# The first forty microseconds of a fused RWKV and feed-forward kernel: a section in written order, dummy products, small loads two at a time, a new list of steps

## The chip, the cores and the metric

The kernel runs on one core of a Trainium2 chip, as one program. The metric is the device time of one execution in microseconds; the time before is the median of three runs. The engines are TensorE (PE, with its weight loads shown as PEld), VectorE (DVE), ScalarE (ACT), GpSimd (POOL) and SyncE (SP), which issues nearly all transfers. All five run their own instruction streams and wait for each other by semaphores.

## What is computed

The reference runs a linear recurrence (RWKV5) over 4 batches, 8 heads, 768 steps and a head size of 48, and feeds its output to a multiplicative feed-forward block:

```
for t in range(S):
    cur = einsum('bhd,bhe->bhde', u * k[t], v[t])
    y[t] = einsum('bhd,bhde->bhe', r[t], state + cur)
    state = w * state + einsum('bhd,bhe->bhde', k[t], v[t])
x = y.transpose(0, 2, 1, 3).reshape(3072, 384)
out = ((x @ w1) * (x @ w2) @ w3) @ w_out
```

The recurrence's inputs are float32. The four weight matrices (384 x 1024 twice, 1024 x 1024, 1024 x 384) arrive as 64-bit floating point words, and the kernel turns them into float32 by integer and shift steps on DVE and ACT.

## The kernel before

**Units.** Time is cut in 6 chunks of 128 steps; a chunk of one batch is a unit n (24 units, unit 0 to 3 are chunk 0). A unit loads k, r and v (three transfers of 192 KB in pieces of 192 bytes), scales k and r by powers of w (`scale`, letter k in the list: one DVE multiplication of 128x768), turns them (T and R: four transposes each on PE with a copy on ACT, t and r; or, for later units, DVE's block transpose x, a transfer to scratch memory y, four transfers back z and a copy l), and makes the pairwise products inside the chunk. U are the additions to the state (32 PE instructions), A the products of r and k (32), S the contribution of the carried state (24 or 48), V the contribution of the pairs (48), Y the copy of the result into `xT`. On DVE, d, e and f make the diagonal term with u, i and j update the state, m masks the products; ACT or DVE (g or h) places the diagonal, and o and p spread the state into a block form.

**Feed-forward.** For each chunk of 512 tokens and each of 8 column blocks j, a.c.j is x @ w1 and b.c.j is x @ w2 (three products of 128x512 each, or 128x256 in two parts for the first blocks), c copies a, u multiplies. w3 and w_out are first multiplied together (G, K, F, X); the last product is done with seven half-size products instead of eight (s and B for the sums, P for the products, E for gathering, D for the store).

**Weights.** W fetches one piece into one of three raw buffers (`raws`); M, N, H, L and Q convert it (ACT, DVE, DVE, ACT, DVE). Pieces 0 to 7 are strips of w1 and w2 in turn; 8 to 15 are w_out; 16 to 31 w3.

**The first section.** Before the units begin, the kernel loads w, computes powers of w up to 32 in both directions in the tile `both`, turns them on PE (`ps_p`, line 274) and copies them to `pn_in` (line 275), by which every unit is scaled. It also tests whether all of w lies in [0.6, 1.6]: a flag that each engine reads, and a branch: inside the range the program runs the list (`program(True)`), outside it another, general path. Only the list is taken here. In the kernel before, w is loaded once more as a row, and DVE takes its minimum and maximum for the flag. The order of this section is left to the scheduler of the language.

**The list.** `ORDER` is a hand-over of an order: a text of steps such as `kr.2 v.2 d.0 W.2`, letter, unit or block, part. `listed()` emits them one by one with the schedule fixed, so each engine executes its own steps in exactly this order, and a step whose input is late holds up all later steps of its engine. Loads (kr, v, W), the turn's transfers (y, z) and the stores (D) all stand in SP's queue in list order.

The buffers that set when transfers can start: three for k and r (`krin`), three for v (`vnat`), three for raw weights (`raws`), two for the scaled k and r (`krs`), two for the turned r (`tts`).

Of the kernel before, what the change touches and what calls it, by code (L numbers as in the profile page):

```python
# [8 lines left out]
F32 = mybir.dt.float32  # L9
# [7 lines left out]
PSUM = bass.MemoryType.PSUM  # L17
PE, ACT, DVE, SP = (getattr(mybir.EngineType, x) for x in ("PE", "Activation", "DVE", "SP"))
# [4 lines left out]
kr.2 v.2 d.0 W.2 N.0 e.0 f.0 M.0 k.0 g.0 H.0 U.0 kr.3 d.1 T.0 k.1 L.0 R.0 e.1 kr.4 t.0 i.0 f.1 r.0 T.1 W.3 Q.0 p.0 A.0  # L23
M.1 h.1 j.0 S.0 t.1 d.2 R.1 k.2 m.0 r.1 R.2 kr.5 e.2 U.1 N.1 r.2 f.2 A.1 M.2 H.1 T.2 i.1 L.1 m.1 V.0 d.3 p.1 W.4 Q.1
v.3 Y.0 t.2 j.1 S.1 g.2 N.2 A.2 k.3 V.1 H.2 R.3 kr.6 Y.1 U.2 m.2 M.3 v.4 T.3 N.3 L.2 a.0.0.0 k.4 r.3 W.5 i.2 a.0.1.0
H.3 p.2 c.0.0.0 e.3 L.3 R.4 j.2 S.2 f.3 M.4 W.6 U.3 Q.3 b.0.0.0 o.4 h.3 c.0.1.0 i.3 t.3 V.2 d.4 p.3 k.5 kr.7 T.4 Y.2
e.4 A.3 v.5 r.4 x.5 S.3 t.4 b.0.1.0 m.3 o.5 y.5 j.3 M.5 V.3 u.0.0.0 u.0.1.0 U.4 f.4 Y.3 v.6 A.4 Q.2 g.4 a.0.0.1 k.6
N.5 b.0.0.1 M.6 N.6 m.4 c.0.0.1 H.6 a.0.1.1 z.5 u.0.0.1 L.6 H.5 b.0.1.1 c.0.1.1 x.6 W.9 L.5 a.0.2.2 u.0.1.1 y.6 i.4
W.8 l.5 Q.6 p.4 d.5 a.0.3.2 Q.5 c.0.2.2 kr.8 j.4 N.4 e.5 S.4 H.4 c.0.3.2 M.8 z.6 U.5 f.5 M.9 V.4 N.8 d.6 L.4 A.5 i.5
kr.9 b.0.2.2 Y.4 h.5 o.6 e.6 W.7 p.5 m.5 v.7 l.6 Q.4 b.0.3.2 j.5 u.0.2.2 N.9 k.7 U.6 f.6 A.6 x.7 g.6 S.5 k.8 y.7 V.5  # L30
d.7 M.7 a.0.4.2 m.6 v.8 kr.10 o.7 e.7 u.0.3.2 Y.5 f.7 z.7 x.8 b.0.4.2 c.0.4.2 d.8 y.8 h.7 kr.11 e.8 i.6 a.0.5.2 f.8
p.6 u.0.4.2 l.7 d.9 j.6 b.0.5.2 c.0.5.2 e.9 H.8 f.9 L.8 H.9 W.11 d.10 L.9 A.7 Q.8 W.12 U.7 u.0.5.2 a.0.6.2 N.7 i.7 H.7
p.7 k.9 L.7 a.0.7.2 j.7 kr.12 c.0.6.2 x.9 W.10 Q.9 y.9 S.6 Q.7 c.0.7.2 z.8 o.8 V.6 m.7 e.10 b.0.6.2 Y.6 g.8 v.9 N.10
N.11 S.7 M.10 f.10 M.11 u.0.6.2 z.9 V.7 o.9 H.10 b.0.7.2 l.8 d.11 Y.7 H.11 v.10 L.10 e.11 L.11 Q.10 W.13 g.9 Q.11 W.14
# [12 lines left out]
y.15 kr.18 K.4.1 f.16 l.14 d.17 M.26 e.17 M.27 H.26 p.13 H.27 L.26 j.13 S.13 L.27 W.29 Q.26 M.28 W.30 V.13 Q.27 o.15
z.15 N.28 A.14 Y.13 H.28 U.14 X.2 m.14 G.5.0 L.28 v.16 G.5.1 i.14 g.15 F.3 W.31 Q.28 N.29 k.16 M.29 f.17 kr.19 p.14
H.29 j.14 L.29 x.16 l.15 Q.29 S.14 y.16 K.5.0 N.30 d.18 X.3 F.4 K.5.1 N.31 e.18 o.16 z.16 G.6.0 X.4 G.6.1 K.6.0 F.5
M.30 K.6.1 H.30 M.31 L.30 H.31 Q.30 L.31 s.1.2.0 Q.31 s.1.2.1 F.6 s.1.0.0 X.5 s.1.2.3 s.1.1.0 s.1.3.0 s.1.1.2 s.1.3.1  # L50
s.1.1.1 s.1.3.3 s.1.3.2 s.1.0.1 s.1.0.2 s.1.0.3 s.1.2.2 G.7.0 X.6 s.1.1.3 U.15 K.7.0 G.7.1 i.15 P.0.0.0 K.7.1 k.17
p.15 F.7 x.17 kr.20 j.15 y.17 A.15 X.7 s.0.1.0 V.14 s.0.0.0 E.0.0.0 l.16 B.0 P.0.1.0 Y.14 v.17 s.0.0.1 g.16 m.15
a.2.1.2 s.0.0.3 B.1 E.0.1.0 f.18 B.2 a.2.2.2 c.2.1.2 B.3 s.0.1.2 s.0.0.2 s.0.2.0 b.2.1.2 d.19 c.2.2.2 s.0.2.2 s.0.2.1
s.0.1.1 s.0.2.3 s.0.3.0 b.2.2.2 s.0.1.3 s.0.3.1 u.2.1.2 s.0.3.3 e.19 s.0.3.2 P.0.0.2 u.2.2.2 P.0.1.2 E.0.0.2 P.0.0.3
E.0.1.2 P.0.0.4 E.0.0.3 P.0.1.3 E.0.0.4 P.0.0.5 E.0.1.3 P.0.1.5 E.0.0.6 E.0.0.5 D.0.0.0 P.0.1.4 E.0.1.6 A.16 E.0.1.4
U.16 E.0.1.5 m.16 D.0.1.0 P.0.0.6 i.16 k.18 p.16 P.0.0.1 j.16 kr.21 S.15 x.18 z.17 o.17 V.15 E.0.0.1 E.0.0.7 U.17 Y.15
a.2.3.2 i.17 g.17 y.18 v.18 k.19 D.0.0.1 kr.22 p.17 f.19 a.2.4.2 l.17 d.20 j.17 c.2.3.2 x.19 e.20 y.19 P.0.1.1 c.2.4.2
P.0.1.6 E.0.1.1 P.1.0.0 E.0.1.7 D.0.1.1 P.1.0.2 E.1.0.0 P.1.0.3 E.1.0.2 P.1.0.4 E.1.0.3 P.1.0.5 E.1.0.4 P.1.1.0
E.1.0.6 E.1.0.5 D.1.0.0 P.1.0.1 E.1.1.0 P.1.0.6 E.1.0.1 P.1.1.1 E.1.0.7 D.1.0.1 P.1.1.2 E.1.1.1 P.1.1.3 E.1.1.2
P.1.1.4 E.1.1.3 b.2.3.2 E.1.1.4 b.2.4.2 u.2.3.2 P.2.0.0 u.2.4.2 s.2.0.0 P.1.1.5 s.2.0.2 E.2.0.0 s.2.0.1 s.2.0.3  # L60
P.2.1.0 E.1.1.5 E.1.1.6 D.1.1.0 P.1.1.6 A.17 E.1.1.7 S.16 D.1.1.1 E.2.1.0 m.17 z.18 o.18 V.16 U.18 g.18 a.2.5.2 i.18
v.19 k.20 p.18 f.20 kr.23 x.20 l.18 a.2.6.2 c.2.5.2 j.18 y.20 d.21 e.21 b.2.5.2 c.2.6.2 a.2.7.2 u.2.5.2 s.2.1.0
s.2.1.2 s.2.1.1 s.2.1.3 b.2.6.2 c.2.7.2 b.2.7.2 u.2.6.2 s.2.2.0 s.2.2.1 s.2.2.2 s.2.2.3 a.3.0.2 Y.16 u.2.7.2 s.2.3.0
s.2.3.1 s.2.3.2 s.2.3.3 b.3.0.2 c.3.0.2 P.2.1.2 u.3.0.2 P.2.0.1 E.2.1.2 P.2.0.2 E.2.0.1 P.2.0.3 E.2.0.2 P.2.0.4
E.2.0.3 P.2.0.5 E.2.0.4 P.2.0.6 E.2.0.5 E.2.0.6 D.2.0.0 P.2.1.3 E.2.0.7 D.2.0.1 P.2.1.4 E.2.1.3 P.2.1.5 E.2.1.4
P.2.1.1 E.2.1.5 E.2.1.6 D.2.1.0 a.3.1.2 E.2.1.1 b.3.1.2 c.3.1.2 P.2.1.6 u.3.1.2 a.3.2.2 E.2.1.7 D.2.1.1 b.3.2.2
c.3.2.2 S.17 u.3.2.2 z.19 o.19 V.17 A.18 Y.17 a.3.3.2 g.19 m.18 v.20 l.19 f.21 b.3.3.2 d.22 c.3.3.2 e.22 A.19 u.3.3.2
U.19 m.19 S.18 i.19 z.20 o.20 V.18 k.21 p.19 a.3.4.2 x.21 g.20 v.21 j.19 y.21 Y.18 P.3.0.0 f.22 l.20 d.23 c.3.4.2 U.20
e.23 E.3.0.0 A.20 i.20 b.3.4.2 k.22 p.20 m.20 x.22 U.21 a.3.5.2 u.3.4.2 y.22 k.23 s.3.0.0 s.3.0.2 s.3.0.1 b.3.5.2
c.3.5.2 s.3.0.3 x.23 a.3.6.2 u.3.5.2 s.3.1.0 s.3.1.2 s.3.1.1 s.3.1.3 b.3.6.2 c.3.6.2 a.3.7.2 u.3.6.2 s.3.2.0 s.3.2.2  # L70
# [21 lines left out]
def kernel(  # L92
# [776 lines left out]
```

## Time and profile before

| | |
|---|---|
| time, median of 3 runs | 515.73 us (515.52 to 516.3) |
| span of the profiled execution | 514.9 us |
| PE busy | 491.7 us |
| DVE busy | 278.0 us |
| ACT busy | 182.9 us |
| bytes moved by the DMA queues | 52.72 MB, 96865 packets, 77729 of them under 512 B |
| k loads, issue to landing | 24 of 192 KB, 4.1 us median |
| r loads | 24 of 192 KB, 4.6 us median |
| weight strips | 8 of 768 KB, 6.3 us median |

Each line of a profile group names the line of the kernel, the engine, the operation, the tile written and the tiles read, with shapes and a count, then the busy time and the mean duration of one. The slices divide the span in 40 equal parts, with the busy share in tenths; PEclk is the clock granted to TensorE. The chain that ended last is followed back from the last instruction: at each step to what released it. "issue" in it is time in which an engine waited for nothing that the profile shows. An f32 product appears as two PE instructions, so three products are "x6".

### The profile page before, as it was taken

Reading aid. Unit: us, or ns where it says so; the run is one execution under the profiler, and the core shown is the slowest. Engines: PE = TensorE matmul, PEld = TensorE weight load, DVE = VectorE, ACT = ScalarE, POOL = GpSimd, SP = SyncE. Lnnn points to the kernel's source line nnn. Section 1 sums busy time; section 2 is a strip of 40 time slices with the busy share of each in tenths; the row PEclk is TensorE's granted clock in tenths of the full one; section 3 lists DMA queues with packets and bytes.
Section 4 is the critical chain, followed back from the end, with each engine's and each line's share of the span. In section 5 each row is a group of like instructions: output and inputs, shape, how many; then the busy total and the mean of one; then the engine's idle time right before and its main releaser. Section 6 shows DMA issues by size and latency. Waiting matters only on the chain.

```text
span 514.9 us, 12195 instructions
## 1 busy us (share of the span) xinstructions
PE 491.7 (95%) x5192; PEld 322.7 (63%) x5192; DVE 278.0 (54%) x587; ACT 182.9 (36%) x455; POOL 6.0 (1%) x23
## 2 busy tenths in 40 slices
PE   1879999999999999999999999999999999999996
PEld 1668555445466666668787477564974754855486
DVE  6869998888376866666325532275322214211342
ACT  3758546766367764402203100341061410001100
POOL 4000000000000000000000000000000000000000
PEclk9979999999999999999999999999999999999999
DMA  7997797768548681303501301220050100000001
GB/s 185 218 232 205 204 240 194 177 230 253 151 101 221 173 223 31 78 1 87 145 32 55 85 0 46 64 83 28 0 140 32 48 2 0 13 19 17 1 17 67
DMA packets 96865, 52.72 MB, mean 102 GB/s; under 512 B 77729, under 2 KB 88226, under 8 KB 96802
## 3 DMA queue, kind: packets, MB, share of 16 engines
q1 hardware_dynamic: 96802, 51.86, 37.4%
q8 instruction: 43, 0.70, 0.6%
q14 instruction: 20, 0.16, 0.1%
HBM read 39.65 MB, written 12.19 MB: 101 GB/s over the span
## 4 chain that ended last, share of the span: by engine, by line
PE 87%; DMA 5%; DVE 2%; SPq 2%; issue 1%; ACT 1%; DVEq 0%; ACTq 0%
PE ps_a L652 23%; PE ps_b L652 22%; PE ps_w L380 8%; PE ps_y L626 3%; PE ps_y L612 3%; PE ps_s4b L709 3%; PE ps_a12b L709 3%; PE ps_a22t L709 3%; PE ps_s2t L709 3%; PE ps_s1t L709 3%; PE ps_s3t L709 3%; PE ps_a11b L709 3%; PE ps_a L512 3%; PE ps_a L505 2%; DMA krin<-in_r_dram 1%; DMA tt<-scratch 1%
## 5 line engine op out<-in xcount | busy, mean ns | idle before, releaser
L652 PE MATMUL ps_a<-xT,w 128*128 128x512 f32 (+1 forms) x300 | 132.5, 585 | 0.0
L652 PE MATMUL ps_b<-xT,w 128*128 128x512 f32 (+1 forms) x300 | 131.0, 578 | 0.5 <-ACT a L658 0.5
L652 PEld LDWEIGHTS ps_b<-xT,w 128*128 128x128 f32 x300 | 56.0, 190 | 63.0 <-issue 56.9
L663 DVE TENSOR_TENSOR abt<-ps_b,a 128x512 f32<-128x512 f32 (+1 forms) x50 | 33.3, 666 | 110.4 <-PE ps_b L652 110.3
L652 PEld LDWEIGHTS ps_a<-xT,w 128*128 128x128 f32 x300 | 56.1, 193 | 57.1 <-issue 53.2
L658 ACT COPY a<-ps_a 128x512 f32<-128x512 f32 (+1 forms) x50 | 28.2, 565 | 129.7 <-PE ps_a L652 124.9
L537 ACT COPY wide<-st 64x192 f32<-64x192 f32 x88 | 30.6, 348 | 59.7 <-PE ps_y L612 27.9
L380 PE MATMUL ps_w<-wo,w3T 128*128 128x384 f32 x128 | 42.5, 487 | 0.0
L419 ACT ACTIVATE AT<-same,dg 128x64 f32<-128x64 f32 x160 | 40.4, 336 | 5.6 <-DVE dg L408 3.2
L380 PEld LDWEIGHTS ps_w<-wo,w3T 128*128 128x128 f32 x128 | 23.9, 190 | 15.7 <-ACT wide L537 0.2
L354 ACT ACTIVATE t<-raw 128x512 uint32<-128x512 uint32 (+2 forms) x32 | 22.4, 707 | 8.0 <-DVE w3n L350 5.2
L626 PE MATMUL ps_y<-AT,vnat 64*64 64x64 f32 x1152 | 23.1, 226 | 1.1 <-issue 1.1
L540 DVE COPY_PREDICATED AT<-later,ps_a 128x512 f32<-128x512 int32 x24 | 17.5, 729 | 10.9 <-PE ps_a L505 6.7
L392 DVE TENSOR_TENSOR krs<-krin,pn_in 128x768 f32<-128x768 f32 x24 | 22.8, 948 | 0.0
L626 PEld LDWEIGHTS ps_y<-AT,vnat 64*64 64x64 f32 x1152 | 19.9, 138 | 4.2 <-issue 2.5
L505 PE MATMUL ps_a<-vnat,krs 64*64 64x48 f32 x704 | 16.8, 224 | 5.9 <-DVE krs L392 3.3
L612 PEld LDWEIGHTS ps_y<-tt,wide 128*32 128x32 f32 x1056 | 16.1, 111 | 9.5 <-issue 5.7
L461 DVE STREAM_TRANSPOSE tr<-krs 128x768 f32<-128x768 f32 x19 | 18.5, 973 | 6.0 <-DMA scratch<-tr 5.9
L612 PE MATMUL ps_y<-tt,wide 128*32 128x64 f32 x1056 | 20.0, 223 | 0.7 <-ACT xT L634 0.7
L505 PEld LDWEIGHTS ps_a<-vnat,krs 64*64 64x64 f32 x704 | 14.3, 139 | 10.1 <-issue 9.6
L512 PEld LDWEIGHTS ps_a<-tt,kT 64*64 64x64 f32 x768 | 14.9, 141 | 8.2 <-issue 4.4
L512 PE MATMUL ps_a<-tt,kT 64*64 64x64 f32 x768 | 18.1, 231 | 1.5 <-issue 0.8
(102 smaller groups left out, 557.3 us busy)
## 6 DMA issues: line engine op xcount, KB each, us to landing
raw<-in_moe_w_dram SPq DMA_DIRECT2D x16, 512.0 KB, 4.8
scratch<-tr SPq DMA_DIRECT2D x19, 384.0 KB, 4.0
raw<-in_moe_w_dram SPq DMA_DIRECT2D x8, 768.0 KB, 6.3
tt<-scratch SPq DMA_DIRECT2D x38, 128.0 KB, 3.1
krin<-in_k_dram SPq DMA_DIRECT2D x24, 192.0 KB, 4.1
krin<-in_r_dram SPq DMA_DIRECT2D x24, 192.0 KB, 4.6
vnat<-in_v_dram SPq DMA_DIRECT2D x24, 192.0 KB, 3.9
raw<-in_moe_w_out_dram SPq DMA_DIRECT2D x8, 384.0 KB, 4.3
```

What stands on the lines that cost most here:

```text
L380: nc.tensor.matmul(ps, lhsT=w3T[j][:, kc, :], rhs=wo[kc], start=(kc == 0), stop=(kc == KF - 1))
L392: nc.vector.tensor_mul(krs[n % NS][:, :, :, :D], kr, pn[:, :, :, :D])
L419: nc.scalar.activation(out=AT[n][:, i, p, :], in_=same, func=COPY, scale=dg[n][:, h:h + 1])
L505: nc.tensor.matmul(added(n)[rows(i), a, p, :], lhsT=kk[rows(a), 2 * p + i, :], rhs=vnat[n % NV][rows(a), 2 * p + i, 0:D], start=True, stop ...
L512: nc.tensor.matmul(upper(n)[rows(a), i, p, :], lhsT=kT[n][rows(i), p, rows(a)], rhs=rT[n][rows(i), p, 2 * a:2 * a + 2], start=True, stop=True)
L537: nc.scalar.copy(out=wide[a][n % 2][rows(i), :, i * D:(i + 1) * D], in_=st[units[n][1]][rows(i)])
L612: nc.tensor.matmul(yt[n][g * Q:(g + 1) * Q, a, q, :], lhsT=wide[a][n % 2][:, p, j * Q:(j + 1) * Q], rhs=rw[:, p, 2 * a:2 * a + 2] if fast ...
L626: nc.tensor.matmul(yt[n][rows(g), a, q, :], lhsT=vv[rows(a), x:x + PAD], rhs=AT[n][rows(a), h % 2, h // 2, :], start=(a, g) not in seen, s ...
L652: nc.tensor.matmul(ps, lhsT=(w1 if x == "a" else w2)[:, z, q, js], rhs=xT[c][:, q, ts], start=(q == 0), stop=(q == KM - 1))
L658: nc.scalar.copy(out=a, in_=ps)
L663: nc.vector.tensor_mul(abt[c, j][:, parts_of_tokens[part]], factor["b", c, j, part], factor["sa", c, j, part])
L709: nc.tensor.matmul(ps, lhsT=of[:, m * C:(m + 1) * C], rhs=w34[:, KH * (x == 1) + j, :DH] if x < 2 else made[b][:, j, :], start=(j == 0), s ...
```

## The change

Five edits, all aimed at the start.

1. **First section in written order.** It stands under the same fixed schedule as the list. The two transfers of the column of w come first, one issued by SP and one by ACT; v of unit 0 goes before the broadcast of u. `both` lies in the third raw weight buffer instead of a tile of its own, and the copy of the second half of the powers goes to ACT.
2. **The path flag by a product with ones.** The row of w is not loaded any more. DVE compares the clamped column with the column itself, PE sums the comparison over partitions by a product with a column of ones, DVE adds four numbers and compares with zero.
3. **Dummy products.** 14 products of a tile of ones at the very start and 12 more behind the flag's product, and in the list the letter Z with a count: six places, 4 + 5 + 5 + 6 + 10 + 11 = 41 products, all before the first feed-forward product. Nothing reads their results. Their purpose is to keep the array from falling idle.
4. **At most two small loads under way.** Each load of k, r or v gets a dependency on the load of k, r or v two before it, so SP waits for that one's landing before it issues.
5. **A new list.** k and r are loaded by steps of their own (kk, rr), the scaling of unit 0 is split in its k and its r half (ka, kb), and all the steps are in another order. The steps themselves are the same, with the same split between the two ways of turning.

```
+ONE_AFTER_THE_OTHER = mybir.DependencyInfo(mybir.DependencyClass.Sync, mybir.DependencyReason.DATA)
 ORDER = """
-kr.2 v.2 d.0 W.2 N.0 e.0 f.0 M.0 k.0 g.0 H.0 U.0 kr.3 d.1 T.0 k.1 L.0 R.0 e.1 kr.4 t.0 i.0 f.1 r.0 T.1 W.3 Q.0 p.0 A.0
-M.1 h.1 j.0 S.0 t.1 d.2 R.1 k.2 m.0 r.1 R.2 kr.5 e.2 U.1 N.1 r.2 f.2 A.1 M.2 H.1 T.2 i.1 L.1 m.1 V.0 d.3 p.1 W.4 Q.1
-v.3 Y.0 t.2 j.1 S.1 g.2 N.2 A.2 k.3 V.1 H.2 R.3 kr.6 Y.1 U.2 m.2 M.3 v.4 T.3 N.3 L.2 a.0.0.0 k.4 r.3 W.5 i.2 a.0.1.0
...
+d.0 ka.0 kb.0 T.0 N.0 M.0 R.0 U.0 Z.4 t.0 H.0 r.0 e.0 L.0 A.0 Z.5 i.0 W.2 f.0 p.0 k.1 v.2 g.0 W.3 S.0 j.0 T.1 Q.0 R.1
+Z.5 d.1 t.1 m.0 M.1 kk.2 e.1 U.1 r.1 N.1 V.0 f.1 i.1 A.1 Z.6 h.1 Y.0 p.1 H.1 M.2 S.1 Z.10 j.1 rr.2 L.1 N.2 m.1 W.4 H.2
+V.1 Z.11 Q.1 L.2 N.3 Y.1 v.3 Q.2 M.3 W.5 a.0.0.0 k.2 kk.3 a.0.1.0 d.2 c.0.0.0 H.3 R.2 e.2 c.0.1.0 b.0.0.0 N.4 L.3 f.2
...
-                nc.sync.dma_start(out=dst, in_=src[b, :, ts, :].rearrange("h t d -> t h d"))
+                small.append(nc.sync.dma_start(out=dst, in_=src[b, :, ts, :].rearrange("h t d -> t h d")))
+                if len(small) > 2:
+                    tc.add_manual_dep(small[-1].ins, small[-3].ins.name, ONE_AFTER_THE_OTHER, reason="few small pieces at a time")
...
-    nc.vector.tensor_reduce(ends[:, 0:1], wrow, AX.X, ALU.min)
-    nc.vector.tensor_reduce(ends[:, 1:2], wrow, AX.X, ALU.max)
-    nc.vector.tensor_scalar(ends[:, 2:3], ends[:, 0:1], W_LOW, None, ALU.is_ge)
-    nc.vector.scalar_tensor_tensor(flag, ends[:, 1:2], W_HIGH, ends[:, 2:3], ALU.is_le, ALU.mult)
...
+    with tc.manual_schedule(engines={PE, ACT, DVE, SP}), tc.tile_pool(name="psW", bufs=2, space=PSUM) as psW:
+        nc.vector.memset(wucol, 1.0)
+        for i, queue in enumerate((nc.sync, nc.scalar)):
+            queue.dma_start(out=wucol[i * PAD:i * PAD + D], in_=w.rearrange("(p i) (d o) -> i d p o", i=2, o=1)[i])
+        load(0, "kr")
+        fetch(0)
+        load(0, "v")
...
+        busy = pn_in[:, 0].rearrange("t h d -> t (h d)")[:, :C]
+        nc.vector.memset(busy, 1.0)
+        def keep_busy(times):
+            for _ in range(times):
+                nc.tensor.matmul(ps_busy, lhsT=busy, rhs=busy, start=True, stop=True)
+        keep_busy(14)
...
+        both = raws[2].bitcast(F32)[:, :2 * NP * C].rearrange("x (g p t) -> x g p t", g=2, p=NP)
...
+                nc.vector.tensor_tensor(outs[:, 0:NP], wn_in[:, 0, 0:NP, 0], wucol[:, :, 0], ALU.not_equal)
+                nc.tensor.matmul(ps_out, lhsT=outs[:, NP:NP + 1], rhs=outs[:, 0:NP], start=True, stop=True)
+                keep_busy(12)
...
+        nc.vector.tensor_copy(out=both[:, 0, :, T:], in_=both[:, 0, :, :T])
+        nc.scalar.copy(out=both[:, 1, :, T:], in_=both[:, 1, :, :T])
+        nc.vector.tensor_reduce(outs[0:1, NP + 1:], ps_out, AX.X, ALU.add)
+        nc.vector.tensor_scalar(flag, outs[0:1, NP + 1:], 0.0, None, ALU.is_equal)
...
+        def busy_array(times):
+            if "busy" not in made:
+                made["busy"] = psF.tile([P, C], F32, tag="f", name="ps_busy")
+            for _ in range(times):
+                nc.tensor.matmul(made["busy"], lhsT=ident, rhs=ident, start=True, stop=True)
```

## The prediction

> **What bounds the kernel now.** I read the page first (engines, then the 40 slices), then busy time by stage, then the chain that ended last in its first 60 us, then the timeline of the first 35 us.
>
> The page: busy time, and slices of 12.9 us.
>
> ```profile
> span 514.9 us, 12195 instructions
> ...
> PE 491.7 (95%) x5192; PEld 322.7 (63%) x5192; DVE 278.0 (54%) x587; ACT 182.9 (36%) x455; POOL 6.0 (1%) x23
> ...
> PE   1879999999999999999999999999999999999996
> ...
> PEclk9979999999999999999999999999999999999999
> DMA  7997797768548681303501301220050100000001
> ```
>
> PE is idle for 23.2 us in all. The stages say where:
>
> ```profile
> 0.00:10.00 10.00, 1.94 (x8) 1.57 (x8) 5.33 (x31) 2.51 (x4) 6.03 (x23) 1.00 0.70 174
> 10.00:20.00 10.00, 6.72 (x104) 5.51 (x104) 9.30 (x17) 7.57 (x18) 0.00 (x0) 1.00 1.04 255
> 20.00:30.00 10.00, 7.57 (x233) 6.42 (x234) 8.20 (x15) 6.63 (x17) 0.00 (x0) 0.83 0.84 197
> 30.00:40.00 10.00, 7.51 (x108) 6.34 (x106) 6.52 (x13) 6.06 (x12) 0.00 (x0) 0.83 0.95 241
> 40.00:60.00 20.00, 20.00 (x427) 14.61 (x425) 18.45 (x33) 13.22 (x31) 0.00 (x0) 1.00 0.77 209
> ```
>
> (Columns: busy PE, PEld, DVE, ACT, POOL, then granted clock, DMA share, GB/s.) The first 40 us hold 16.3 us of the idle time, the tail after the last product about 4, and all between only 2.9. So a change of the start is worth what it moves the moment from which PE never rests, now about 32.5 us, and later edits can give back at most 2.9. The chain through the start, then its instructions:
>
> ```profile
> 7.58 1.96 PE ps_p L274 x8
> ...
> 16.86 7.68 DMA krin<-in_r_dram
> ...
> 30.02 2.49 issue
> 32.51 0.82 PE ps_a L505 x27
> 33.34 1.04 PE ps_kT L439 x4
> 34.38 3.59 PE ps_a L652 x12
> 37.98 0.44 PE ps_rT L439 x4
> ```
>
> ```profile
> 9.62 0.56 DVE L401 TENSOR_TENSOR ruk<-krin 128x384 f32<-128x384 f32 x1 [1.98 <-PE ps_p L274]
> ...
> 11.62 0.95 DVE L392 TENSOR_TENSOR krs<-krin,pn_in 128x768 f32<-128x768 f32 x1
> ...
> 13.86 1.11 PE L439 MATMUL ps_kT<-ident,krs 128*128 128x128 f32 x4
> ...
> 24.52 0.46 PE L626 MATMUL ps_y<-AT,vnat 64*64 64x64 f32 x14 [1.15 <-issue]
> ```
>
> Three things are to be seen. DVE sits idle 1.98 us until the power transposes end, and `krs` of unit 0 comes only at 11.62, so the first turn (T.0) starts at 13.86. The array runs at half speed: four transposes take 1.04 to 1.11 us at 13.86 and 33.34, 0.44 at 37.98. And PE stops in the middle of a group for no semaphore ("issue": 1.15 us after 34 of 48 products, 2.49 us after 5 of 32); during the longer stop DVE idles too (4.49 us).
>
> [...] granted 0.54 in 26.4 to 29.7 us, 0.96 to 33.1, 0.53 to 36.5, then 1.00. Before the first recorded event the clock column says 1.00 although eight transposes took 1.94 us, so there durations decide. [...] the two stops lie at PE instruction 437 and 691, 254 apart. [...]
>
> **The change part by part.** *Where break-even lies.* I compare the start of the first feed-forward product (a.0.0.0). Before: 34.38, and its 12 products took 3.59 where 2.58 (twice 1.29) is the full-clock time, 1.0 lost. The new list puts R.2, T.2, R.3, T.3 (4 x 0.44), U.2 (0.61) and A.2 (0.62) behind it, which stood before it: 3.0 us of PE work still to do. So the new kernel gains whatever it starts that product before 34.4 + 1.0 - 3.0 = 32.4 us; from there the product work is the same.
>
> *First section.* The row of w is no longer loaded (one issue of 0.35 us) and the two columns go out on two queues: the column, which landed at 3.49, should land at 3.0. Then DVE's chain 3.59 to 7.14 (3.55), the comparison (0.17 to 0.2) and one copy (0.30; the other is now ACT's, beside it): powers ready at 7.1. The flag costs one product and two tiny DVE steps, about 0.4 us, beside PE's transposes: nothing. `both` now lies in a weight buffer, so DVE's 1.98 us wait goes; the third weight load waits instead, behind a branch that SP reaches only at 11 to 12.
>
> *26 early dummies.* One is two passes of 128 columns: six passes of 256 take 1.29, so 0.215 us at full clock, 0.43 at half. They start at about 1.1. [...] all 26 end at 8.4 or 10.1; I take 9.2. This is later than 7.1: they hold the transposes up by 2 us. These then take 1.0 in place of 1.94, and the copies (0.58 each) make `pn_in` ready at 10.4 and 10.95, against 9.29 and 10.14. Alone this part loses about 1 us.
>
> *Written order after the branch.* DVE does d.0, then the k half of the scale (about 0.5), so T.0 starts at 11.0 in place of 13.86. DVE's list from there to m.1 (unit 1's mask): ka, kb 1.0; N, H, Q of the first weight 2.45; N, H of the second 1.5; N of the third 0.55; e, f twice 2.2; k.1 0.95; d.1 0.55; i, j twice 2.16; m twice 1.46; h.1 0.68; sum 13.5, less 0.08 overlap for 23 instructions: 11.7. From 10.45 that is 22.2; with 0.8 for waits on PE and ACT (U.0 before i.0, the eight `AT` copies of 2.02 before m.0) 23.0. V.1 (0.86) ends at 24.0, the 11 dummies behind it (2.4) at 26.4. PE's own list agrees: four turns 1.76, U twice 1.2, A twice 1.24, S twice 0.94, V twice 1.72, so 6.9 us of real work, and 41 dummies of 0.215 (8.8) from 11.0 make 26.7. The dummies fill idle time, except the last 11, which may cost up to 1 us.
>
> [...] Their stops were 1.15 and 2.49; bounds 0 and 3.6, I take 1.5. First product at 28.
>
> *Two small loads at a time.* On SP everything queues behind a waiting load: weights, and the `tr`/`tt` transfers, on which ACT's kT waits. Landings of before: k and r of unit 0 after 3.1 and 3.3 us, the median under load 5.3 to 5.6. With 3.1 to 4 each, r1 lands near 13.5, v1 16.5, k2 22, r2 23, in time for k.1 (14), U.1 (17) and k.2 (26). With 5.6 each, r2 lands at 28, about when k.2 wants it. By bytes, loads up to the fourth weight are 4.7 MB, 19 us at 250 GB/s: landed at 22. So nothing, with up to 2 us as the bad end.
>
> *The new list later.* From 40 to 80 us DVE is busy 37.2 of 40, so PE's lead holds only if DVE gets ahead too. DVE idled 6.3 us between 9.6 and 40; the packed order can give most of that. The rest has 2.9 us of PE idle before; I take it unchanged.
>
> Sum: 32.4 - 28 = 4.4 us; 515.7 - 4.4 = 511.3.
>
> **Rivals.** *The wait comes back elsewhere.* [...] a late r2 (1 to 2): 32.4 - 31.5, about 1 us gained: 514.8. For it: DMA share is 0.84 to 1.04 in the start, and the small loads are still as many. Against: the weights are far ahead (fourth weight at 22, wanted near 48). *Slower.* Gated loads hold up the `tr`/`tt` transfers and DVE is nearly full, so PE loses 1 us in each of eight units between 80 and 200 us, where DMA share is 0.63 to 0.81: 511.3 + 8 = 519.3. Against: DMA waits there fall on ACT (kT, 4.5 us in 150 to 200), and PE idles 0.8. *More.* [...] half of the 2.9 gone: 26.4, so 6 + 1.5: 508.2.
>
> **How the numbers follow.** Main case 0.62 (508.5 to 514), wait elsewhere 0.18 (514 to 516), slower 0.13, more 0.07. Predicted 511.3. The range 508.3 to 516.0 keeps the main case and the first rival and leaves out the slower one and the best. Faster by over 0.2% (below 514.7): 0.62 + 0.07 + 0.08 of the first rival = 0.77; within 0.2%: 0.10; slower 0.13.
>
> **What would show it.** Right: transposes of the powers at 8.4 to 10.1 and taking about 1.0 us; T.0 near 11; groups of four transposes near 0.44 from then on; a.0.0.0 at 26.5 to 29.5 and PE without rest from there; idle between there and the tail under 4 us. Wrong: a.0.0.0 after 32, long waits on the small loads at SP with PE idle behind them, or new PE idle beyond 60 us.

## The result, and the profile after

The kernel after takes 523.05 us (median of four runs, 521.62 to 523.87) against 515.62 beside it: ratio 1.0149, 95% interval 1.0108 to 1.019. It is slower by 1.5%, where 511.3 us was forecast.

The page of the kernel after: span, busy time, then rows of the 40 slices.

```profile
span 522.1 us, 12477 instructions
...
PE 505.2 (97%) x5328; PEld 337.0 (65%) x5328; DVE 278.6 (53%) x588; ACT 183.2 (35%) x456; POOL 6.0 (1%) x23
...
PE   8997998999999999999998999999999999999996
...
PEclk9999998999999999999999999999999999999999
```

PE is busy 13.5 us longer and idle 16.9 us where it was idle 23.2. That looks better and isn't: 19.6 us of the busy time are dummies, which do none of the kernel's own work. The time in which PE does no work of the kernel's own is 16.9 + 19.6 = 36.5 us, against 23.2. The busy time by stage (PE, PEld, DVE, ACT, POOL, granted clock, DMA share, GB/s):

```profile
0.00:10.00 10.00, 8.85 (x55) 8.70 (x56) 4.76 (x31) 1.89 (x3) 6.03 (x23) 1.00 0.70 178
10.00:20.00 10.00, 8.60 (x154) 7.56 (x153) 7.50 (x14) 8.06 (x19) 0.00 (x0) 1.00 1.02 303
20.00:30.00 10.00, 9.70 (x239) 9.12 (x234) 9.93 (x18) 5.46 (x9) 0.00 (x0) 1.00 0.65 177
30.00:40.00 10.00, 8.88 (x130) 7.39 (x128) 7.15 (x14) 7.19 (x19) 0.00 (x0) 1.00 0.75 197
40.00:60.00 20.00, 17.18 (x232) 11.27 (x231) 18.67 (x33) 13.29 (x28) 0.00 (x0) 1.00 0.84 212
...
80.00:100.00 20.00, 17.11 (x465) 11.41 (x464) 15.50 (x33) 10.55 (x28) 0.00 (x0) 0.91 0.70 153
```

Before, PE had no idle time between 40 and 60 us; now it has 2.8, and between 80 and 100 it has 2.9 (0.5 before), where the clock falls too. PE's timeline of the start (start, duration, instruction; in brackets the idle time before it and what ended that):

```profile
1.15 6.01 PE L256 MATMUL ps_busy<-pn_in 128*128 128x128 f32 x28 [1.15 <-DVE raw L265]
...
7.21 2.94 PE L256 MATMUL ps_busy<-pn_in 128*128 128x128 f32 x24
9.99 1.04 PE L293 MATMUL ps_p<-ident,raw 128*128 128x128 f32 x8
11.95 0.63 PE L458 MATMUL ps_kT<-ident,krs 128*128 128x128 f32 x4 [0.92 <-DVE krs L411]
...
24.15 2.50 PE L768 MATMUL ps_busy<-ident 128*128 128x128 f32 x20
26.58 0.93 PE L645 MATMUL ps_y<-AT,vnat 64*64 64x64 f32 x48
27.44 2.72 PE L768 MATMUL ps_busy<-ident 128*128 128x128 f32 x22
30.00 2.76 PE L671 MATMUL ps_a<-xT,w 128*128 128x256 f32 x12
```

The powers were ready at about 7.2, but their turns stand behind 12 dummies until 9.99. From T.0 at 11.95 the array runs at full clock (granted 1.00 from 6.66 to 85.17 us). The mask of unit 1 ended at 24.62 on DVE, so V.1 could have started there; the ten dummies of Z.10 (20 passes, since each is two PE instructions) hold it until 26.58. The copy of xT ended at 28.08; Z.11 holds the first product, a.0.0.0, until 30.00. PE executes in list order, and none of these waits shows as idle.

Behind the first product PE stops, which it did not before:

```profile
33.03 1.46 PE L671 MATMUL ps_b<-xT,w 128*128 128x256 f32 x6
...
35.52 1.46 PE L671 MATMUL ps_b<-xT,w 128*128 128x256 f32 x6
...
37.39 0.69 PE L531 MATMUL ps_a<-tt,kT 64*64 64x64 f32 x32
39.21 0.63 PE L458 MATMUL ps_rT<-ident,krs 128*128 128x128 f32 x4 [1.12 <-DVE krs L411]
...
43.07 0.91 PE L631 MATMUL ps_y<-tt,wide 128*32 128x64 f32 x24 [0.86 <-ACT wide L556]
44.79 0.93 PE L645 MATMUL ps_y<-AT,vnat 64*64 64x64 f32 x48 [0.81 <-DVE AT L559]
46.34 1.56 PE L671 MATMUL ps_a<-xT,w 128*128 128x256 f32 x6 [0.62 <-ACT xT L653]
```

The steps of units 2 and 3 hang from each other through PE, ACT and DVE in turn. Before, products of the feed-forward part lay between them, as the timeline of the kernel before shows:

```profile
39.42 1.56 PE L652 MATMUL ps_b<-xT,w 128*128 128x256 f32 x6
40.92 0.93 PE L626 MATMUL ps_y<-AT,vnat 64*64 64x64 f32 x48
...
42.99 0.54 PE L612 MATMUL ps_y<-tt,wide 128*32 128x64 f32 x24
43.46 1.56 PE L652 MATMUL ps_b<-xT,w 128*128 128x256 f32 x6
44.95 0.93 PE L626 MATMUL ps_y<-AT,vnat 64*64 64x64 f32 x48
```

In the kernel after both of these products are over at 36.98, and none is left to fill the gaps up to 46.34.

I compare at three marks: a.0.0.0; a.0.2.2, the first product on all 512 tokens, which needs units 0 to 3; and the end.

| profiled run | a.0.0.0 starts | from there to a.0.2.2 (PE idle) | a.0.2.2 starts | from there to the end (PE idle) |
|---|---|---|---|---|
| before | 34.18 | 17.98 (0.0) | 52.16 | 462.74 (6.9) |
| after | 30.00 | 22.34 (3.9) | 52.34 | 469.76 (10.2) |

The start gained 4.18 us, all of it was gone at a.0.2.2, and 7.0 were lost behind it, 2.1 of them for products that the new list has still to do there.

### The profile page after: what moved, and what is told of

It is laid out like the page before. It is cut to its first block, busy times and chain, and to the rows that moved or that the text cites. A ratio compares the mean times of both kernels' runs of the same rounds, so it can differ in the third digit from the quotient of the medians.

```text
span 522.1 us, 12477 instructions
## 1 busy us (share of the span) xinstructions
PE 505.2 (97%) x5328; PEld 337.0 (65%) x5328; DVE 278.6 (53%) x588; ACT 183.2 (35%) x456; POOL 6.0 (1%) x23
## 3 DMA queue, kind: packets, MB, share of 16 engines
q1 hardware_dynamic: 96592, 51.85, 36.5%
## 4 chain that ended last, share of the span: by engine, by line
PE 87%; DMA 5%; DVE 2%; ACT 2%; SPq 1%; issue 1%; ACTq 0%; DVEq 0%
PE ps_b L671 23%; PE ps_a L671 22%; PE ps_w L399 6%; PE ps_y L631 3%; PE ps_s3t L728 3%; PE ps_s2t L728 3%; PE ps_y L645 3%; PE ps_a22t L728 3%; PE ps_a12b L728 3%; PE ps_a L531 3%; PE ps_s4b L728 3%; PE ps_s1t L728 3%; DMA tt<-scratch 3%; PE ps_a11b L728 3%; PE ps_a L524 2%; PE ps_busy L256 2%
## 5 line engine op out<-in xcount | busy, mean ns | idle before, releaser
L682 DVE TENSOR_TENSOR abt<-ps_b,a 128x512 f32<-128x512 f32 (+1 forms) x50 | 33.4, 669 | 108.6 <-PE ps_b L671 104.6
L411 DVE TENSOR_TENSOR krs<-krin,pn_in 128x768 f32<-128x768 f32 (+1 forms) x25 | 22.9, 920 | 2.5 <-ACT pn_in L294 2.2
L497 ACT COPY kT<-tt 128x512 f32<-128x512 f32 x19 | 11.8, 619 | 26.8 <-DMA tt<-scratch 22.5
L524 PEld LDWEIGHTS ps_a<-vnat,krs 64*64 64x64 f32 x704 | 13.5, 134 | 7.8 <-issue 6.1
```

The lines of the kernel that those rows point to most:

```text
L411: nc.vector.tensor_mul(krs[n % NS][:, which, :, :D], kr[:, which], pn[:, which, :, :D])
L524: nc.tensor.matmul(added(n)[rows(i), a, p, :], lhsT=kk[rows(a), 2 * p + i, :], rhs=vnat[n % NV][rows(a), 2 * p + i, 0:D], start=True, stop ...
L682: nc.vector.tensor_mul(abt[c, j][:, parts_of_tokens[part]], factor["b", c, j, part], factor["sa", c, j, part])
```

## The experiments

Ratios are to the kernel before, run on the same chip beside each group. "e1" and so on are short for the names in full.

### Which edit costs the time: four runs

e1_no_gate is the kernel after without the limit on small loads.

```
-                if len(small) > 2:
+                if False:
```

> The changed kernel without the limit of two small loads. Theory A (the limit holds up SP, and with it the weights and the tt transfers behind it): the 23 us that SP waits for small loads between 30 and 120 us go away, TensorE's idle time between the first product and the tail falls from 11 us to about 3, and the time falls by some 8 us, to 513 to 517. Theory B (the new list itself places steps so that tt comes late, whatever SP waits for): the stops on kT stay, 520 to 524.

Measured: 520.97 us, ratio 1.0141 (1.01 to 1.0181). By the medians the limit costs 2 us, by the ratios (1.0149 with it) 0.4: little, and not told apart from nothing. PE's stop at 83 us, 2.3 us long, stays without it.

e2_old_with_gate is the other side: the kernel before with the limit alone (the `if len(small) > 2` block added to its load).

> The kernel before with the limit of two small loads alone. Theory A: SP stands behind small loads here too, and TensorE idles several us more: 519 to 526. Theory B: the limit costs little, 514 to 517.

Measured: 518.7 us, 1.0082 (1.0043 to 1.012): 3.8 us slower by the medians. The limit is no help in either kernel.

e3_old_with_new_list is the kernel before with the new list, its Z, ka and kb included, without the limit and with the old first section.

```
 ORDER = """
-kr.2 v.2 d.0 W.2 N.0 e.0 f.0 M.0 k.0 ...
+d.0 ka.0 kb.0 T.0 N.0 M.0 R.0 U.0 Z.4 ...
```

> The kernel before with the new list alone (its 41 dummies and the split scaling of unit 0 are part of it), no limit, the old first section. Theory A: the list is sound without the limit, and its dummies keep the array at full clock: 511 to 516. Theory B: the list is what costs, and without the new first section it starts some 1 to 3 us later as well: 521 to 526.

Measured: 524.97 us, 1.0207 (1.0166 to 1.0247). The list alone, with its dummies, costs 10 us.

e4_new_start_old_list is the kernel after with the old list (no Z in it) and no limit: new first section and 26 early dummies.

> The new first section with its 26 early dummies, the old list, no limit. If the first section is worth what the new trace shows (T.0 at 11.95 in place of 13.86), 512 to 515 under both theories. If the old list's start is bound by its small loads [...], 515 to 517.

Measured: 513.75 us, 0.9983 (0.9959 to 1.0007). So the new first section isn't told apart from the old one, and the new list loses. Between e1 and e4, which differ in the list alone, the spans are 518.8 and 511.5 us. e4 starts a.0.2.2 at 49.32 and e1 at 51.36, with T.4, R.4, U.4 and A.4 (2.1 us) still to do: e1 is 4.1 us behind there, and the rest has 9.4 us of PE idle against 6.6, 2.8 more. Together 6.9 of the 7.3. The 4.1 us are there before the first product: e4 starts a.0.0.0 at 27.98 and e1 at 29.74, with 3.0 us of other products still to do, so 4.8 us behind. Between the two marks both idle alike (3.9 and 3.5 us). Neither the clock nor stops that nothing released ("issue" in a timeline's brackets) make the difference: the clock's record is at full from 5.2 to 510.4 us in e4 and from 6.1 to 518.1 in e1, and such stops of 0.3 us or more add up to 4.2 us in e4 and 1.4 in e1.

### Where in the list: two hybrids

Both have the new first section and no limit; their list is the new one up to a step and the old order from there.

> New first section, no limit; the new list up to the first feed-forward product, from there the remaining steps in the old order. Theory C (the new list loses what it leaves behind the first products: units 2 and 3 run as one dense chain after 35 us, with nothing beside it): the old order spreads that chain between products, so about 513 to 516. Theory D (the new list's first 30 us, with 41 dummies, are themselves too long): little changes against the whole new list, 518 to 521.

Measured, e5_new_list_to_first_product (new up to a.0.0.0): 519.35 us, 1.0098 (1.007 to 1.0127). It tells less than I wanted. In the old order unit 3's turns stand ahead of a.0.0.0, and the new list fetches its k and r after W.2 to W.5: R.3 waits 3.14 us for the scaled r, and a.0.0.0 starts at 38.34.

> The same with the new list up to the first product of chunk 1, some 110 us in, then the old order. Theory C: the loss of 35 to 50 us is in it, 516 to 519. Theory E (the loss is in the tt waits after 110 us): 513 to 515.

Measured, e6_new_list_to_chunk_1 (new up to a.1.0.2, the first product of the second chunk): 520.28 us, 1.0149 (1.0092 to 1.0206), as slow as e1. PE is idle for 3.5 us from 30 to 50 and 2.6 us from 80 to 100. So the part up to a.1.0.2, some 100 us, is enough for the loss. It doesn't clear the order behind it: from a.1.0.2 to the end e6 needs 417.5 us in its trace and e1 419.2, and e6 lost as much ahead of it to half clock (45.9 to 49.3 us), which e1 doesn't have.

### The best version

e7_old_list_v3_early_no_12: e4 without the 12 dummies ahead of the power turns, and with v of unit 3 fetched before W.4. In e4 PE had waited 1.9 us for that v.

```
-                keep_busy(12)
...
-d.3 p.1 W.4 Q.1 v.3 Y.0
+d.3 p.1 v.3 W.4 Q.1 Y.0
```

> A try for a better kernel: new first section without the 12 dummies that stand before the transposes of the powers, no limit, the old list with the load of v of unit 3 moved in front of the fifth weight load. The transposes go from 9.3 to about 7.2 us, and the stop for v of unit 3 (its landing at 33.4 us ended the chain in the run with the old list) shrinks by up to 3 us: 509 to 512. If the clock falls back without the 12 dummies, 512 to 515.

Measured: 510.94 us, 0.9936 (0.9914 to 0.9958). It beats both kernels. Its trace has no stop of 0.3 us or more that nothing released, where e4 has five with 4.2 us, so this pair doesn't say what the 12 dummies or v.3 alone are worth.

### The dummies

e8_no_dummies takes all 67 dummies out of the kernel after and keeps its limit and its order.

> The changed kernel without any dummy product, all else kept. If the dummies pay by holding the clock: slower than with them by 1 to 4 us, 524 to 527. If they cost (the 12 before the transposes hold back the start by 2.8 us, the 11 before the first product by about 2): faster, 519 to 522.

Measured: 526.1 us, 1.0248 (1.0216 to 1.0281): slower than the kernel after by 3 us in the medians and 5 in the ratios. PE's timeline of e8:

```profile
7.29 1.94 PE L291 MATMUL ps_p<-ident,raw 128*128 128x128 f32 x8 [3.12 <-DVE outs L286]
10.05 1.09 PE L456 MATMUL ps_kT<-ident,krs 128*128 128x128 f32 x4 [0.83 <-ACT pn_in L292]
...
27.41 5.49 PE L669 MATMUL ps_a<-xT,w 128*128 128x256 f32 x12 [0.61 <-ACT xT L651]
```

T.0 comes 1.9 us and a.0.0.0 2.6 us earlier than in the kernel after, but the array is at half clock (by the record from 23.1 to 33.4 us, and again from 47.0 to 50.4): the first twelve passes take 5.49 us where they took 2.76. The dummies delay, and pay by the clock.

e9_short_dummies_in_list keeps them and cuts only the last two groups.

```
-S.1 Z.10 j.1 rr.2 L.1 N.2 m.1 W.4 H.2 V.1 Z.11
+S.1 Z.2 j.1 rr.2 L.1 N.2 m.1 W.4 H.2 V.1 Z.2
```

> The kernel after with the two last groups of dummies in the list cut from 20 and 22 passes to 4 each, nothing else. In the kernel after they kept V.1 and then a.0.0.0 from starting for about 2 us each while both were ready, and their copies delay L.3 and Q.3, from which units 2 and 3 hang. Theory A (the long dummies are a cause of their own, and the start they hold back carries through): a.0.0.0 starts at 27.5 to 28.5 us where it started at 30.0, and the time is 519.5 to 521. Theory B (the new list is late for what comes after it, whenever the first product starts; the small-piece loads of units 2 and 3 set the pace there): a.0.0.0 starts earlier all the same, a stop of the same size appears behind it between 30 and 50 us, and the time stays at 522 to 523.5.

Measured: 522.23 us, 1.0149 (1.0096 to 1.0201). a.0.0.0 starts at 26.69, 3.3 us earlier, and the time isn't told apart from that of the kernel after (0.8 us by the medians). In the trace the lead is there for long: 3.2 us at a.0.2.2, and 3.8 at a.1.0.2 (98.27 against 102.10). Of these, 2.0 are lost behind it, where e9 has four stops that nothing released (4.5 us together, at 170.9, 186.4, 210.1 and 278.0) and the kernel after none of 0.3 us or more.

### The stop at 84 us

The chain of the kernel after through this stop (start, length, what):

```profile
76.03 0.33 SPq L225
...
77.37 1.49 SPq L492
...
78.91 4.59 DMA tt<-scratch
...
83.57 0.63 ACT kT L497
...
84.24 0.79 PE ps_a L531 x31
```

z.6, the transfer of unit 6's turned k and r, stands on SP behind the weights W.15 and W.16. In e10_z6_ahead_of_weights it stands ahead of them; nothing else is changed.

```
-e.7 H.12 f.7 L.12 U.5 H.13 W.15 A.5 M.14 d.8 L.13 i.5 V.4 W.16 k.7 p.5 a.0.6.2 z.6
+e.7 H.12 f.7 L.12 U.5 H.13 z.6 W.15 A.5 M.14 d.8 L.13 i.5 V.4 W.16 k.7 p.5 a.0.6.2
```

> The kernel after with one token moved: z.6, the transfer of the turned k and r of unit 6, stands ahead of W.15 in SP's queue instead of behind W.16. In the kernel after it was issued at 76.5 us and landed at 83.5, and PE stopped for 2.6 us at 84 us for it, and then ran some 3.4 us at half clock. Theory A (this stop is a loss of its own): no stop over 1 us between 80 and 90 us, clock 0.98 or more there, and the time falls by 2.5 to 4 us to 519 to 520.5. Theory B (the stop only collects what is lost anyhow, since the loads behind it come later): a stop of like size appears at W.15, W.16 or another unit within 20 us, and the time stays at 522 to 523.5.

Measured: 525.35 us, 1.0183 (1.0133 to 1.0234), not faster, and by the intervals not told apart from the kernel after. The chain of e10 at the same place:

```profile
78.56 5.10 DMA raw<-in_moe_w_dram
83.66 0.02 issue
83.69 0.02 ACT w3n L361
...
84.82 0.53 ACT kT L497
85.39 1.23 PE ps_a L531 x24
```

z.6 now waits on SP until 75.19, and the weights wait behind it. On ACT the conversion of W.16 stands ahead of the copy of kT, so ACT waits for the weight in place of z.6, and PE stops for 3.8 us in place of 2.6. So moving this one step doesn't take the stop away.

e11_new_list_mended undoes four things in the kernel after together: the limit, the 12 dummies ahead of the power turns, the length of Z.10 and Z.11 (as in e9), and the place of z.6 (as in e10).

> The kernel after with four things undone together: no limit on the small loads, no 12 dummies ahead of the turns of the powers, the last two groups of dummies cut to 4 passes each, and z.6 ahead of W.15. If the losses seen one by one add up (limit 2, dummies 2 to 3, the stop at 84 us 2.5 to 4), the new list comes to 513.5 to 516.5 us, level with the kernel before. If the list's order of units 2 and 3 is the rest of the loss, it stays at 517.5 to 520.5.

Measured: 520.88 us, 1.0109 (1.0065 to 1.0153). a.0.0.0 starts at 24.28, 5.7 us earlier than in the kernel after; a.0.2.2 at 50.97, only 1.4 earlier. The losses seen one by one did not add up in the time, but other losses came in their place. From 38.6 to 48.8 us e11 is at half clock, where e1, e9 and the kernel after are not:

```profile
42.63 2.92 PE L670 MATMUL ps_a<-xT,w 128*128 128x256 f32 x6 [0.62 <-ACT xT L652]
45.35 2.77 PE L670 MATMUL ps_b<-xT,w 128*128 128x256 f32 x6
```

The same two take 1.56 and 1.46 us in e9; over the five groups of this stretch it makes 4.1 us, so most of the lead of 5.7. The mean clock of the four executions is 0.988 to 0.993, against 0.996 to 1.0 in e1. Stops that nothing released take 3.0 us, where e1 has 1.4. So this run doesn't show that the order of units 2 and 3 is the rest of the loss.

### Does the first product count?

e12_old_list_unit_0_first is e7 with another start of the list.

```
-kk.2 rr.2 v.2 d.0 W.2 N.0 e.0 f.0 M.0 k.0 g.0 H.0 U.0 kk.3 rr.3 d.1 T.0 k.1 L.0 R.0 ...
+kk.2 rr.2 v.2 ka.0 kb.0 T.0 U.0 R.0 W.2 d.0 M.0 t.0 i.0 N.0 r.0 Z.3 p.0 A.0 k.1 T.1 ...
```

> The best kernel so far (new first section without the 12 dummies, no limit, the old list with v.3 ahead of W.4; 510.9 us) with the start of the list put in another order: unit 0 is scaled and turned as soon as its powers are there, ahead of the first weights, six dummies fill PE before A.0, and the weights M.2 go behind the copy Y.0 on ACT. That kernel had PE idle for 4.1 us ahead of its first turn (waiting for the scaling, which stood behind six operations on DVE) and for 2.7 us at V.1's products (ACT waiting for the raw weights of M.2). If both stops go and the rest follows, a.0.0.0 starts at 23.5 to 25.5 us where it started at 28.8, and the time is 505.5 to 508.5. If the landings of k, r and v of units 2 and 3 take the place of the stops, the time is 509.5 to 511.5.

Measured: 512.92 us, 0.9954 (0.9934 to 0.9974), not told apart from e7. T.0 starts at 9.33 where e7 started it at 13.08; then PE waits 5.8 us for DVE and is back at half clock (granted 0.74 from 20 to 30 us; four transposes take 1.08 us at 19.95 where they took 0.63 at 9.33). a.0.0.0 starts at 30.43, later than the 28.82 of e7, and a.0.2.2 at 48.70 against 48.47.

e15_units_0_and_1_first goes further: in e7's list, units 0 and 1 stand ahead of all weights but W.0, and a.0.0.0 and a.0.1.0 ahead of most of unit 2. The diagonals of units 0 and 1 also change engines (h.0 for g.0, g.1 for h.1).

```
+... A.1 d.1 e.1 f.1 g.1 N.0 i.1 p.1 S.1 H.0 L.0 m.1 j.1 V.1 kk.4 rr.4 Q.0 W.3 Y.1 M.1 k.2 a.0.0.0 ...
```

> The old list's start (new first section without the 12 dummies, no limit, v.3 ahead of W.4) put in another order: on DVE units 0 and 1 stand ahead of all weights but W.0, and the products a.0.0.0 and a.0.1.0, which need W.0 alone, ahead of unit 2. DVE has some 11 us of work ahead of the first product then, where it had 19. If the first product is what counts and DVE's order sets it, it starts at 21 to 23.5 us (28.8 in the best kernel so far) and the time is 505 to 508.5 us. If what counts is the sum of the work on DVE up to units 2 and 3 and the first weights, or their landing, the products stop behind it and a.0.2.2 starts at 47.5 to 49 us again: 509.5 to 512.5 us.

Measured: 517.11 us, 1.0033 (1.0014 to 1.0052), slower than e7 by 1%. PE's timeline of e15:

```profile
22.67 2.93 PE L670 MATMUL ps_a<-xT,w 128*128 128x256 f32 x6 [0.60 <-ACT xT L652]
...
33.98 0.93 PE L644 MATMUL ps_y<-AT,vnat 64*64 64x64 f32 x48 [1.95 <-DVE AT L558]
...
38.77 0.64 PE L457 MATMUL ps_rT<-ident,krs 128*128 128x128 f32 x4 [2.07 <-ACT tt L467]
42.50 1.11 PE L457 MATMUL ps_kT<-ident,krs 128*128 128x128 f32 x4 [3.09 <-ACT kT L464]
...
54.79 1.45 PE L670 MATMUL ps_a<-xT,w 128*128 128x512 f32 x3
```

The first product comes 6.2 us earlier than in e7, and PE stops three times behind it, for 7.1 us, with half clock from 19.5 to 26.4 and from 40.0 to 46.8 us. a.0.2.2 comes 6.3 us later, of which 3.0 are made up by the end. The marks of all these kernels:

| kernel | list | a.0.0.0 | a.0.2.2 | from there to the end |
|---|---|---|---|---|
| before | old | 34.18 | 52.16 | 462.74 |
| e4 | old | 27.98 | 49.32 | 462.18 |
| e7 | old | 28.82 | 48.47 | 462.93 |
| e12 | old, start changed | 30.43 | 48.70 | 462.00 |
| e15 | old, start changed | 22.67 | 54.79 | 459.91 |
| after | new | 30.00 | 52.34 | 469.76 |
| e1 | new | 29.74 | 51.36 | 467.44 |
| e9 | new, short Z | 26.69 | 49.15 | 471.15 |
| e11 | new, mended | 24.28 | 50.97 | 467.43 |

The first column doesn't order the others, and a lead or delay in the second doesn't carry whole to the end (e9, e15). Whatever its start, the new list needs 467 to 471 us from a.0.2.2 (2.1 of it the work it has left), the old one in this table up to 463.

### Which half of the list: an exchange that did not answer

Both kernels have the new first section and no limit; steps on PE, DVE and ACT keep one list's order and the transfers take the other's, each as early as its buffers allow. The lines show transfers alone: "-" in the order made for that work, "+" as run.

```
 e13, work of the old list
-kk.2 rr.2 v.2 W.2 kk.3 rr.3 kk.4 rr.4 W.3 kk.5 rr.5 W.4 v.3
+W.2 v.2 W.3 kk.2 rr.2 W.4 v.3 kk.3 rr.3 W.5 kk.4 rr.4 W.6
 e14, work of the new list
-W.2 v.2 W.3 kk.2 rr.2 W.4 v.3 W.5 kk.3 rr.3 W.6 kk.5 rr.5
+kk.2 rr.2 v.2 W.2 kk.3 rr.3 kk.4 rr.4 W.3 kk.5 rr.5 W.4 v.3
```

> New first section and early dummies, no limit, the old list (as the kernel that ran in 513.75 us), but with the transfers of the new list: the tokens of k, r, v, the weights and the turned blocks stand in the order in which the new list issues them, everything on PE, DVE and ACT stays in the old order. Theory A (the new list loses by its order of transfers, which puts weights ahead of the k, r and v of units 2 and 3): most of the 7 us go with the transfers, 518 to 521 us. Theory B (it loses by its order of work on PE, DVE and ACT): 513 to 515.5 us, as with the old transfers. In between, 515.5 to 518, both have a share.

> The other half of the exchange: the kernel after without the limit (520.97 us), its list's order of work on PE, DVE and ACT kept, dummies included, and the transfers put into the order of the old list up to about 50 us (W.5, W.7 and W.8 a little earlier, where the work needs them). Theory A (order of transfers): 513 to 516 us, with the stops between 38 and 47 us and at 83 us gone. Theory B (order of work): 519.5 to 522 us and the stops stay. In between both have a share.

Measured: e13_old_list_new_transfers 595.46 us, 1.1534 (1.1465 to 1.1604); e14_new_list_old_transfers 580.44 us, 1.1236 (1.117 to 1.1303). Neither theory expected this. In e13 PE waits for v (19.1 us), the scaled r (11.9) and kT (9.7); in e14 for the spread state (10.9) and others. Each order of work ran some 80 (e13 against e4) and 60 us (e14 against e1) longer with the transfers of the other, so this pair can't say which half of the new list loses.

### What sets the pace up to a.0.2.2

In before, after, e1, e4, e7, e9, e11, e12 and e15, DVE is busy 35.2 to 36.9 us between its first operation on a unit and a.0.2.2, so I suspected DVE. Three changes to e7 test it: more work on DVE, more on PE, less on DVE.

```
 e16
-            nc.vector.tensor_reduce(dg[n], ruk[n], AX.X, ALU.add)
+            for _ in range(3 if n < 4 else 1):
+                nc.vector.tensor_reduce(dg[n], ruk[n], AX.X, ALU.add)
 e17, in turn_k
+                for _ in range(3 if n < 4 and g == 0 else 1):
 e18, in the list
-h.1 ... h.3
+g.1 ... g.3
```

> The best kernel (new first section without the 12 dummies, no limit, old list with v.3 ahead of W.4; 510.9 us, ratio 0.9936) with 4.4 us more of work on DVE in its first 50 us: the sums f of units 0 to 3 are taken three times each (eight more of 0.55 us). Theory C (DVE sets the pace up to a.0.2.2: in nine kernels it had 35.2 to 36.9 us of work there, whichever list, and 4 to 9.5 us idle): a.0.2.2 starts 3 to 4.5 us later, at 51.5 to 53, and the time is 513.5 to 515.5 us. Theory D (the order of events on PE sets it): under 1.5 us, up to 512.5.

> The twin of the run before: the same best kernel with 4.9 us more of work on PE in its first 50 us, the turns T of units 0 to 3 three times each (32 passes more). Theory C: PE has 11 us idle there, so most of it is hidden: a.0.2.2 at 48.5 to 50 us, 511 to 512.5 us. Theory D: a.0.2.2 4 to 5 us later, 514.5 to 516 us.

> The best kernel with the diagonals of units 1 and 3 made on ACT (g, 2.0 us each) where DVE made them (h, 0.7 us each): 1.4 us less on DVE in the first 50 us, 4.0 us more on ACT. Theory C, if ACT has room: 0.5 to 1.5 us faster, 509.5 to 510.5. If ACT, which also copies what the units turn, becomes the wait: 511 to 514 us.

Measured: e16_dve_4us_more 0.9956 (0.994 to 0.9973), so 1.0 us over e7's 0.9936 and not told apart from it, with a.0.2.2 at 49.95; e17_pe_5us_more 1.0057 (1.0036 to 1.0078), 6.2 us over e7, with a.0.2.2 at 53.50; e18_diagonals_on_act 0.9975 (0.9956 to 0.9994), 2.0 us over e7, with a.0.2.2 at 53.18. (The medians are 513.26, 517.88 and 513.91 us; the kernel before was 515.3 in that group.) My theory fell: DVE took most of 4.4 us more from its own idle time, and taking 1.4 us away made it slower; in its trace PE waits 3.0 us for a copy of ACT at 40.2, with half clock from 39.1 to 45.9. The run with more on PE is not clean: beside the added turns (4.3 us in the trace) it has two long stops that nothing in the trace releases, 3.31 and 2.29 us, where e7 has none, and half clock from 47.4 to 50.8. PE's timeline of e17:

```profile
46.14 0.46 PE L531 MATMUL ps_a<-tt,kT 64*64 64x64 f32 x14 [3.31 <-issue]
...
71.87 0.33 PE L645 MATMUL ps_y<-AT,vnat 64*64 64x64 f32 x2 [2.29 <-issue]
```

So DVE alone doesn't set this stage. I read it as a chain that passes through PE, ACT and DVE, which these runs don't prove.

## Why the prediction was wrong

**The step that failed** is "from there the product work is the same", with "The rest has 2.9 us of PE idle before; I take it unchanged." I measured the gain at the first product, and put what the new list does behind it at nothing. In the profiled runs the start won 4.18 us (the timeline's 34.18 to 30.00; my 34.38 was the chain's). Against it stand the 3.0 us of work moved behind the first product, less the 1.0 of half clock that went: so 2.2 of gain by my own account. Then came 3.9 us of new idle time up to a.0.2.2, 3.2 behind it, and about 1.4 of half clock around the stop at 84 us (granted 0.65 from 84 to 88). That is -2.2 + 3.9 + 3.2 + 1.4 = 6.3 of the 7.2 us between the two spans; 0.9 I can't place. The runs show that it was the list: the old one behind the same start is 7.3 us shorter (e4 against e1).

They also show that the mark was the wrong one. By the same account, with 1.0 of half clock gone and no work moved, the old list behind the same start has 7.2 us of gain at its first product (27.98, e4), and its time is 1.2 us shorter by the medians. And an earlier first product alone did not show in the time: 3.3 us (e9) and 5.7 us (e11) brought 0.8 and 2.2 us by the medians, within the noise, and in their traces much of the lead goes to half clock and to stops that nothing released. 6.2 us by another order (e15) cost 1%.

The other steps:

- *First section.* Right: powers ready at 7.2 (7.1 forecast), the flag free. With the old list, without the 12 dummies and with v.3 earlier it is worth 0.6% (e7).
- *Early dummies.* Nearly right: the turns of the powers end at 11.0 where I had 10.2. When the clock would come was my estimate, which no trace of before shows; it came at 6.65. The flag's product and the passes themselves (0.116 us from start to start, where I took 0.108) add to the delay. Their price, a loss of about 1 us taken alone, is not measured: e4 and e7 differ by 2.4 us for the 12, v.3 and e4's stops together. I left out what all dummies together are for: without them the kernel is 3 to 5 us slower, with half clock from 23.1 to 33.4 and from 47.0 to 50.4 us (e8).
- *Dummies in the list.* Mis-sized: "except the last 11, which may cost up to 1 us" was 1.96 us for Z.10 and 1.9 for Z.11. The sum had Z.11 in full, but not Z.10. With unit 1's mask at 24.6 in place of 23.0 this makes 26.4 + 1.6 + 2.0 = 30.0; the forecast of 28 was 26.4 and 1.5 for stops that nothing releases. e9 takes 3.3 us of it back and keeps them up to a.1.0.2, so by the traces these dummies are part of the loss; the times can't confirm it.
- *DVE's idle time* between 9.6 and 40 us was 6.0 us by the windows, not 6.3; nothing hangs on it.
- *Stops that nothing releases.* I reserved 1.5 us for them before the first product, an estimate from the two in the trace of before (1.15 and 2.49); behind the start of the dummies PE waits there for nothing longer than 0.92 us. That was luck: with the 1.5 us of stops the first product would have come at 31.5.
- *Two small loads at a time.* I took nothing, "with up to 2 us as the bad end". It is 0.4 to 2 us with the new list and 3.8 with the old, outside my bounds.
- *The rival that ended slower* had the right side and the wrong cause. It foresaw 519.3 us from gated loads that hold up the turned blocks. One such stop is in the trace, at 84 us, but it stays without the limit (2.3 us, e1), and moving z.6 makes it longer (3.8, e10).

What the runs leave open: which steps of the new list, within its first 100 us, cost the 7 us. The two long groups of dummies are a part (e9). That the products a and b were used up before unit 3's chain was through is what the timelines of after and e15 show side by side with the stops; no run moved only those products, and e4 idles as long in this stretch (3.9 us, for v and in stops that nothing released) and is faster, so it isn't proved as the cause. Nor is it known why the new list has 2.8 us more idle time behind a.0.2.2.

## What to carry to other kernels

When work is moved ahead in an order that a whole pipeline shares, count at each mark what is done and what is left, and follow it to the end: here neither the first product nor a.0.2.2 told the time. Count dummy work as idle time, and place it where nothing that is ready stands behind it on the same engine. Look in each trace for half clock and for stops that nothing released before a difference is put down to the edit. And try each edit of a bundle alone on the old order first: here the start, without its 12 dummies and with v.3 earlier, was worth keeping (e7), and the list and the limit were not.

## What the hardware showed that I had not expected

- The clock took 5.5 us of unbroken dummies to be released in the kernel after: the passes follow each other every 0.21 us from 1.15 to 6.65, and every 0.11 behind that, and the record of full clock starts at 6.66. Behind the same 14 dummies it starts at 5.2 us in e4 and at 6.1 in e1, some 4.0 and 4.9 us after the first dummy. A plan for this kernel can't take one figure for it: these three took 4.0 to 5.5 us.
- The traces of before and after show how busy PE was when the clock changed. Between the start of the clock's record (19.22 us in before, 6.66 in after) and the tail they have three stretches of half clock, each 3.41 us long: 26.04 to 29.46 and 32.87 to 36.28 us in before, 85.17 to 88.58 in after. In the 3.41 us ahead of each, PE was busy for 1.59, 0.92 and 0.93 us; within them, up to the return of full clock, for 3.11, 3.41 and 3.41. Full clock held through 19.22 to 22.63 us of before with PE busy for 2.66. Three falls make no threshold.
- PE can stop where nothing in the trace releases it. Before has three such stops of 0.5 us or more: 1.15 us behind 449 of PE's instructions (products, weight loads and those of its sequencer), 2.49 behind 705 and 0.80 (at 172.58 us) behind 4802. (The 437 and 691 of the prediction leave out 12 and 14 of the sequencer's, so that 256 came out as 254.) After passes 449 and 705 without a stop of 0.3 us, and has one of 0.32 us (at 98.91) behind 3009. What stops PE there is not shown. Such stops come and go with an edit: e17's two long ones took 5.6 us, and e7, with 32 passes fewer, has none of 0.3 us or more.
- With the limit of two small loads under way, the median landing of r was 3.5 us where it is 4.4 without it (e1), and of k 3.6 where it is 4.1, and it gained nothing: against e1 the kernel after has no lead, and e2 lost 3.8 us. In the kernel after, SP's waits from 30 to 120 us (total, times, longest):

```profile
SPq L204 <- DMA vnat<-in_v_dram: 10.8, 5, 3.3
...
SPq L204 <- DMA krin<-in_k_dram: 9.1, 6, 3.0
...
SPq L204 <- DMA krin<-in_r_dram: 3.1, 2, 1.8
```

That is 23.0 us in which SP could issue nothing else. But SP stands about as long without the limit, for buffers in place of landings: all its waits in this stretch add up to 56 us here, 50 in e1, 59 in the kernel before and 56 in e2. So the 23 us are not the price of the limit, and why e2 lost 3.8 us stays open.
